# Dense 16-bit results from VectorE's last pass over its score blocks, with part of the work on GpSimd

## The chip, the cores and the metric

The kernel runs on one core of a Trainium2 chip. The time is device microseconds of one execution; a kernel's figure is the median of its runs. Five engines work side by side: TensorE (PE, with its weight loads as PEld), VectorE (DVE), ScalarE (ACT), GpSimd (POOL) and SyncE (SP), which here only issues DMA transfers.

## The reference

Two independent parts are computed and concatenated. Part A is multi-head attention with 32 heads of 16 channels over 2048 positions; part B is a long causal convolution with a gate.

```python
qkv = x @ wqkv                                   # A: x is 2048 x 512
scores = einsum("bhqd,bhkd->bhqk", q, k) * Dh**-0.5
p = softmax(scores)
a = einsum("bhqk,bhkd->bhqd", p, v) @ wo
k_shift = sum over 4 taps of shifted k * shift_k # B
kv = k_shift * v
y = causal convolution of kv with ssm_k (length 2048) + kv * ssm_D
b = q * y
return concatenate([a, b], axis=-1)              # bfloat16, 1 x 2048 x 1024
```

The exponentials of part A are 32 x 2048 x 2048 numbers. The kernel cuts them into 2048 **blocks** of 128 keys by 512 queries.

## The kernel before

**Chunks.** The program is written out by a planner that runs when the kernel is built. It walks over 695 chunks (index T). A chunk has two or three score blocks, each in a PSUM bank of its own: `emit_qk` issues one matmul for each block (L756) and then one ScalarE activation, exp from PSUM to the bf16 tile `PT` (L763). There are two groups of three banks, and odd and even chunks take turns. The matmuls of chunk T+1 may start when each of its banks is free, and a bank is free when its exp, or VectorE's first read of it, is done. Later `emit_pv` multiplies each block of exponentials with the values (L930).

**Who makes the exponentials.** ScalarE makes most of them. In some chunks `dve_choice` gives the last block to VectorE; ScalarE's activation then covers 1024 columns and not 1536 (in the first 56 chunks every second one has only two blocks to begin with). `dve_choice` says no where the planner's own clock has VectorE too far behind (`FIX_BEHIND`, `LATE`, `OPEN_LATE`), where a set was begun too recently (`OPEN_STEPS`, `APART`), or where the place for a result is still in use.

**How VectorE makes an exponential.** The scores come scaled so that a power of two has 2^16 steps. The block is first read out of PSUM as an int32 fixed-point number (`exp_on_dve`, L784, "fix" below; tiles `EI` and, later, a part of `xT`). After that it works on **sets** of two or four blocks (`Set`, `passes`), in SBUF:

- L815 `to_frac`: the low 16 bits, as f16: the fraction f. GpSimd makes it one block at a time where the planner finds a slot, otherwise VectorE does.
- L880, L882, L883, L885: four passes over the whole set, with f16 tiles (`EA`, or the lent tiles `WKV`, `STG`, `xT`, `YB`): a cubic correction with its two roots near 0 and 1.
- L886: the last pass, in pieces of half a set: the int32 number times 128, plus the correction, written back as int32. Its upper 16 bits are the bf16 exponential, and L930 reads every second 16-bit word.

**What sets the order.** Every engine takes its instructions in the order that the planner wrote. VectorE's fixes come when their chunk does. The passes wait in a list (`dve_fill`) from which the planner takes one whenever it thinks VectorE would be idle, and at the latest when the set's results are due. `free_slot` hands GpSimd one job for each VectorE instruction of about 0.69 us that reads PSUM (two for one of 1.24 us), with a wait for the VectorE instruction two places earlier; so a job stands ready when such an instruction begins. GpSimd's jobs are L815 and the softmax division L959. Other names in the profile: L484, L465, L510, L450, L1000, L1048, L1129 and L1147 are VectorE's reads of other matmul results, L536 and L542 prepare the convolution, L1116 is the convolution's matmul, L1293 and L1311 are matmuls with zeros that only fill TensorE's time.

Of the kernel before, what the change touches and what calls it, by code (L numbers as in the profile page):

```python
# [17 lines left out]
QB = 512  # L18
# [24 lines left out]
N_EARLY = 56  # L43
LAGS = 5
CONV_AT = 128
CONV_END = 650
TAIL = 18

OCT = 2.0 ** 16
ROOT0, ROOT1 = 0.0127173909, 0.9900476185
C0, C1 = 0.3043078141, 0.0780240431
FS = 128.0
BITS = 2.0 ** 23
QSCALE = SCALE * math.log2(math.e) * OCT
FIX_LO = -118.0 * OCT
FIX_ADD = 127.0 * OCT
# [28 lines left out]
HARD = 0.7  # L88
# [14 lines left out]
KZ_AT = 11  # L103
KZ0_AT = 14
DG_AT = (1, 1, 7, 8)
V_DUE = 1
PACE = 0.9
FULL_PARTS = 6
KZ_LANDS = 24.2
# [105 lines left out]
def bass_concat_heads__mha_block__ssm_conv_h3__prompt_kernel(  # L215
# [442 lines left out]
    def ei_of(off, n=1):  # L658
        return EI[:, off:off + n, :] if off < 8 else EIC[:, off - 8:off - 8 + n, :]
# [131 lines left out]
            full(s)  # L791
        return s.fix[-1]

    pool_jobs, waiting = [], []

    def full(s):
        if not s.pool:
# [15 lines left out]

    def to_frac(e, out, src):
        return e.tensor_scalar(out, src.bitcast(UINT16).rearrange("p i (f e) -> p i f e", e=2)[:, :, :, 0],  # L815
                               FS / OCT, -FS * ROOT0, ALU.mult, ALU.add)

    class Job:

# [3 lines left out]
    def frac_job(s, i):  # L823
        def run(eng, deps):
            _, eb, old = bufs(s)
            s.frac[i] = pool.op(lambda e: to_frac(e, eb[:, i:i + 1, :], ei_of(s.off + i)), deps + [s.fix[i], h_set[s.w]] + old, us=POOL_US)
            if s in waiting and len(s.frac) == s.k:
                passes(s)
        pool_jobs.append(Job(s, s.fix[i], lambda: not s.before or all(b in h_blk for b in s.before.blks), run))

    def free_slot(us=0.69):
        if us < 0.65:
            return
        n = dve.n - 2
        pool.t = max(pool.t, dve.t - us + DVE_OVER)
        for _ in range(int(us / 0.6)):
            j = next((j for j in pool_jobs if j.dep[1] <= n and j.ready()), None)
            if j:
                pool_jobs.remove(j)
                j.run(pool, [(dve.sem, n)])  # L840
                dve.t = max(dve.t, pool.t)

    def passes(s):
        ei = ei_of(s.off, s.k)
        ea, eb, old = bufs(s)
        eg = ea.bitcast(BF16)
# [9 lines left out]
        def piece(rate, make, deps, i0, i1, ends):  # L856
            us = 0.155 + 0.533 * (i1 - i0) / rate

            def run():
                h = dve.op(make(slice(i0, i1)), [st.get(i, h_set[s.w]) for i in range(i0, i1)] + (deps() if callable(deps) else deps), us=us, fill=True)  # L860
                for i in range(i0, i1):
                    st[i] = h
                if ends:
                    h_set[s.w] = h_ea[s.ea] = h
                    for x in s.blks[i0:i1]:
                        h_blk[x] = h
            return us, run, due, s

        def step(rate, make, deps=(), ends=False):
            width = s.k if s.pool and not ends else (s.k + 1) // 2  # L870
            for i0 in range(0, s.k, width):
                new.append(piece(rate, make, deps if callable(deps) else list(deps), i0, min(i0 + width, s.k), ends))

        make = lambda sl: lambda e: to_frac(e, eb[:, sl], ei[:, sl])
        if not s.frac:
            step(2, make, s.fix + old)
        for i in range(s.k):
            if s.frac and i not in s.frac:
                new.append(piece(2, make, s.fix + old, i, i + 1, False))
        step(4, lambda sl: lambda e: e.tensor_scalar(ea[:, sl], eb[:, sl], FS * (ROOT0 - ROOT1), None, ALU.add),  # L880
             lambda: [h_set[s.w], h_ea[s.ea]] + old)
        step(2, lambda sl: lambda e: e.tensor_tensor(ea[:, sl], ea[:, sl], eb[:, sl], ALU.mult))  # L882
        step(4, lambda sl: lambda e: e.tensor_scalar(eb[:, sl], eb[:, sl], C1 * BITS / FS ** 3,  # L883
                                                     (C0 + C1 * ROOT0) * BITS / FS ** 2, ALU.mult, ALU.add))
        step(2, lambda sl: lambda e: e.tensor_tensor(eg[:, sl], ea[:, sl], eb[:, sl], ALU.mult))  # L885
        step(1, lambda sl: lambda e: e.scalar_tensor_tensor(ei[:, sl], ei[:, sl], BITS / OCT, eg[:, sl], ALU.mult, ALU.add),  # L886
             ends=True)
# [26 lines left out]
    def emit_pv(bl, T):  # L914
# [676 lines left out]
```

## Time and profile before

| | |
|---|---|
| runs shown | 815.08, 816.94, 818.94 us; median 816.94 us |
| profiled execution | 814.36 us, of which the profile's span is 812.6 us |
| ACT busy | 796.1 us, 98% of the span, 702 instructions |
| DVE busy | 775.1 us, 95%, 1078 instructions |
| PE busy | 706.1 us, 87% |
| POOL busy | 354.9 us, 44%, 344 instructions |
| granted TensorE clock | full speed throughout |

A row of the groups reads: line, engine, operation, tiles written and read, shapes, count | total busy us, mean ns of one | idle time of the engine just before these instructions, and what ended it. Two instructions that follow each other on an engine overlap a little in these records, so durations add up to slightly more than time. A row of the timeline begins with start and duration in us.

### The profile page before, as it was taken

The page shows a single profiled execution, that of the slowest core. Times are in us where ns is not written, and L with a number is a line of the kernel's source. Part 1 is how long each engine was busy: PE and PEld are TensorE (multiplying, and loading weights), DVE is VectorE, ACT ScalarE, POOL GpSimd, SP SyncE. Part 2 cuts the span into 40 slices and gives each one's busy share as a digit, 9 for nine tenths or more (in the row PEclk, how much of TensorE's full clock was granted, in tenths as well). Part 3 has the DMA queues.
Part 4 walks back from the last instruction along what each step waited for, and adds up shares of the span by engine and source line. Part 5 has one row for each costly group of instructions (what it writes and reads, how often), then busy time and mean ns, then how long its engine had stood idle before and what let it go on. Part 6 is the DMA issues. An engine that isn't in the chain of part 4 may idle for free.

```text
span 812.6 us, 30077 instructions
## 1 busy us (share of the span) xinstructions
PE 706.1 (87%) x13348; PEld 316.5 (39%) x13383; DVE 775.1 (95%) x1078; ACT 796.1 (98%) x702; POOL 354.9 (44%) x344
## 2 busy tenths in 40 slices
PE   8998889888888889888888888888888888888897
PEld 3333334333334433343434343344444444344432
DVE  4999999999999999999999999999999999999996
ACT  7999999999999999999999999999999999999996
POOL 4202223244444464645534534345465556545450
PEclk9999999999999999999999999999999999999999
DMA  9986601115468775668767687787898999658810
GB/s 247 284 328 215 183 1 26 52 27 141 151 193 253 225 231 184 191 208 288 225 195 244 217 273 237 221 272 240 263 289 253 294 314 292 201 164 274 286 28 27
DMA packets 125010, 167.33 MB, mean 206 GB/s; under 512 B 50384, under 2 KB 57040, under 8 KB 124624
## 3 DMA queue, kind: packets, MB, share of 16 engines
q1 hardware_dynamic: 122480, 164.34, 65.8%
q8 instruction: 106, 1.74, 0.9%
q10 hardware_dynamic: 2400, 1.05, 0.5%
q14 instruction: 24, 0.20, 0.1%
HBM read 143.14 MB, written 16.52 MB: 196 GB/s over the span
## 4 chain that ended last, share of the span: by engine, by line
ACT 84%; DVE 8%; PE 6%; DMA 1%; issue 1%; POOL 0%; DVEq 0%
ACT PT L763 84%; PE PS L756 2%; DVE EI L886 1%; DVE EI L784 1%; PE PS L930 1%; DMA WR<-kz_scratch 1%; PE PS L474 1%; DVE EA L880 1%; DVE VAF L484 1%; DMA KV<-in_A_x_dram 1%; DVE WR L536 1%; DVE EA L882 0%; PE PS L498 0%; DVE EA L885 0%; DVE KV L510 0%
## 5 line engine op out<-in xcount | busy, mean ns | idle before, releaser
L763 ACT ACTIVATE PT<-PS 128x1024 bf16<-128x1024 f32 (+1 forms) x695 | 792.1, 1450 | 4.8 <-PE PS L756 4.0
L756 PE MATMUL PS<-QT,KTo 32*128 32x512 bf16 x2048 | 272.0, 384 | 89.8 <-ACT PT L763 63.1
L930 PE MATMUL PS<-PT,VAF 128*32 128x512 bf16 x1748 | 232.4, 389 | 2.0 <-DVE STG L1000 1.7
L1116 PE MATMUL PS<-WR,KV 128*18 128x64 bf16 (+15 forms) x8192 | 186.6, 213 | 1.3 <-DMA WR<-kz_scratch 0.8
L1116 PEld LDWEIGHTS PS<-WR,KV 128*18 128x18 bf16 (+15 forms) x8192 | 150.7, 119 | 40.4 <-issue 18.5
L756 PEld LDWEIGHTS PS<-QT,KTo 32*128 32x128 bf16 x2048 | 69.7, 91 | 241.0 <-ACT PT L763 215.7
L815 POOL TENSOR_SCALAR xT<-EI 128x512 f16<-128x512 uint16 x88 | 107.2, 1218 | 106.6 <-DVE EI L886 28.6
L784 DVE TENSOR_SCALAR EI<-PS 128x512 int32<-128x512 f32 x220 | 150.2, 684 | 3.7 <-PE PS L756 3.5
L815 POOL TENSOR_SCALAR STG<-EI 128x512 f16<-128x512 uint16 x76 | 84.1, 1106 | 86.6 <-DVE EI L886 23.3
L930 PEld LDWEIGHTS PS<-PT,VAF 128*32 128x32 bf16 x1748 | 55.2, 93 | 91.1 <-issue 84.0
L886 DVE SCALAR_TENSOR_TENSOR EI<-EI,EA 128x1024 int32<-128x1024 int32 (+1 forms) x92 | 90.2, 989 | 0.5
L815 POOL TENSOR_SCALAR xT<-xT 128x512 f16<-128x512 uint16 x40 | 43.7, 1092 | 47.0 <-DVE EI L886 25.7
L815 POOL TENSOR_SCALAR STG<-xT 128x512 f16<-128x512 uint16 x40 | 42.1, 1051 | 44.0 <-DVE EI L886 25.2
L1293 PE MATMUL PS<-ZR,IDN 128*128 128x512 bf16 (+3 forms) x217 | 59.3, 325 | 0.0
L930 PE MATMUL PS<-EI,VAF 128*32 128x512 bf16 x220 | 54.1, 406 | 2.0 <-DVE VAF L484 1.5
L784 DVE TENSOR_SCALAR xT<-PS 128x512 int32<-128x512 f32 x80 | 54.7, 684 | 0.2 <-PE PS L756 0.2
L886 DVE SCALAR_TENSOR_TENSOR EI<-EI,WKV 128x1024 int32<-128x1024 int32 x38 | 46.0, 1213 | 0.1
L882 DVE TENSOR_TENSOR EA<-EA,xT 128x2048 f16<-128x2048 f16 x32 | 39.7, 1240 | 0.3
L885 DVE TENSOR_TENSOR EA<-EA,xT 128x2048 bf16<-128x2048 f16 x32 | 39.0, 1220 | 0.4
L815 POOL TENSOR_SCALAR YB<-EI 128x512 f16<-128x512 uint16 x18 | 13.8, 767 | 54.2 <-DVE EI L784 30.9
L815 POOL TENSOR_SCALAR EA<-EI 128x512 f16<-128x512 uint16 x20 | 15.9, 794 | 48.8 <-DVE EI L784 10.4
L885 DVE TENSOR_TENSOR WKV<-WKV,STG 128x2048 bf16<-128x2048 f16 x29 | 35.3, 1219 | 0.5
(100 smaller groups left out, 644.1 us busy)
## 6 DMA issues: line engine op xcount, KB each, us to landing
WR<-kz_scratch SPq DMA_DIRECT2D x512, 256.0 KB, 3.8
kz_scratch<-WR SPq DMA_DIRECT2D x16, 752.0 KB, 4.3
QN<-in_B_q_dram SPq DMA_DIRECT2D x16, 128.0 KB, 3.3
out_dram<-KV SPq DMA_DIRECT2D x16, 128.0 KB, 4.0
out_dram<-OUTA SPq DMA_DIRECT2D x12, 128.0 KB, 1.9
QT<-in_B_ssm_k_dram SPq DMA_DIRECT2D x1, 1024.0 KB, 5.6
EI<-in_B_ssm_k_dram SPq DMA_DIRECT2D x1, 1024.0 KB, 8.8
STG<-in_B_v_dram SPq DMA_DIRECT2D x1, 1024.0 KB, 7.2
```

Source lines behind the costliest of these rows:

```text
L474: ins = e.matmul(PS[:, bank, 256 * i:256 * i + 256], lhsT=xT[:, dc, (kt + i) * 128:(kt + i + 1) * 128], rhs=WV[:, dc, 256 * z:256 * z + 25 ...
L484: bank_free[bank] = hh = dve.op(lambda e: e.tensor_copy(dst, src), [h, h_vaf1])
L756: ins = e.matmul(PS[:, bank, :], lhsT=KTo[32 * s:32 * s + 32, g // 2, kt * 128:(kt + 1) * 128], rhs=QT[32 * s:32 * s + 32, qb % 2, g, :], ...
L763: h_exp[T] = act.op(lambda e: e.activation(PT[:, T % R_PT, 0:n * QB], PS[:, banks[0]:banks[0] + n, :].rearrange("p b f -> p (b f)"), ACT.E ...
L784: s.fix.append(dve.op(lambda e: e.tensor_scalar(ei_of(i)[:, 0, :], PS[:, bank, :], FIX_LO, FIX_ADD, ALU.max, ALU.add), [h] + old + [o.pv[i ...
L815: return e.tensor_scalar(out, src.bitcast(UINT16).rearrange("p i (f e) -> p i f e", e=2)[:, :, :, 0], FS / OCT, -FS * ROOT0, ALU.mult, ALU ...
L882: step(2, lambda sl: lambda e: e.tensor_tensor(ea[:, sl], ea[:, sl], eb[:, sl], ALU.mult))
L885: step(2, lambda sl: lambda e: e.tensor_tensor(eg[:, sl], ea[:, sl], eb[:, sl], ALU.mult))
L886: step(1, lambda sl: lambda e: e.scalar_tensor_tensor(ei[:, sl], ei[:, sl], BITS / OCT, eg[:, sl], ALU.mult, ALU.add), ends=True)
L930: ins = e.matmul(PS[32 * s:32 * s + 32, pvb(qb * NG + g), :], lhsT=VAF[:, kt, h * VW:h * VW + 32], rhs=rhs, start=(order[b] == 0), stop=(o ...
L1116: ins = e.matmul(PS[32 * c:32 * c + NW - 2 * n, BGB, col:col + 64], lhsT=KV[:, 2 * n:NW, 4 * qd + c], rhs=w, start=(n == 0), stop=(n == NB ...
L1293: return e.matmul(PS[:, bank, col:col + 128 * k], lhsT=IDN[:, :], rhs=ZR[:, :].rearrange("p (m d) -> p m d", m=1).broadcast_to([128, 4 * k ...
```

## The change

The last pass no longer keeps the linear part of the number in int32. The four passes make the whole mantissa as a cubic in the fraction, f(C1 + f(C2 + f C3)), scaled to 128 steps, and the last pass adds the integer part times 128 and writes a dense int16 row, which is the bit pattern of the bf16 exponential (the first half of the block's int32 row). L966, the matmul with the values, reads that dense row.

The integer part is the upper 16 bits of the fixed-point number. It gets to the last pass in one of two ways. Where the planner finds a GpSimd slot before the last pass is issued, GpSimd makes the integer part times 128 as f16, one block at a time and in place (`to_whole`, L834; these `whole_jobs` come after `pool_jobs` in `free_slot`), and the last pass is a plain `tensor_tensor` add of two f16 rows (L884). Otherwise it is a `scalar_tensor_tensor` that reads the upper words itself (L889). If a piece has one block of each kind, it is cut into single blocks. Some of the planner's constants have new values.

```diff
-CONV_END = 650
+CONV_END = 640
-OPEN_STEPS = 4
+OPEN_STEPS = 5
-LATE = 8.0
+LATE = 9.0
-PAIRS_AT_END = 18
+PAIRS_AT_END = 20
-OPEN_LATE = 4.0
+OPEN_LATE = 5.0
-FIX_BEHIND = 1.6
+FIX_BEHIND = 1.7
-FIX_LATE = 0.4
+FIX_LATE = 0.45
-V_DUE = 1
+V_DUE = 0
-POOL_WAIT = 8
+POOL_WAIT = 7
+FINISH_RATE = 1.8
-X2_AT = 140
-X1_AT = 162
+X2_AT = 146
+X1_AT = 166
...
     def to_frac(e, out, src):
         return e.tensor_scalar(out, src.bitcast(UINT16).rearrange("p i (f e) -> p i f e", e=2)[:, :, :, 0],
-                               FS / OCT, -FS * ROOT0, ALU.mult, ALU.add)
+                               FS / OCT, None, ALU.mult)
...
+    def to_whole(e, out, src):
+        return e.tensor_scalar(out.bitcast(FP16)[:, :, 0:QB], src.bitcast(UINT16).rearrange("p i (f e) -> p i f e", e=2)[:, :, :, 1],
+                               FS, None, ALU.mult)
+
+    def whole_job(s, i, dep):
+        def run(eng, deps):
+            s.whole[i] = pool.op(lambda e: to_whole(e, ei_of(s.off + i), ei_of(s.off + i)),
+                                 deps + [dep, s.frac.get(i)], us=POOL_US)
+        whole_jobs.append(Job(s, dep, lambda: True, run))
...
-            j = next((j for j in pool_jobs if j.dep[1] <= n and j.ready()), None)
+            j = next((j for j in pool_jobs + whole_jobs if j.dep[1] <= n and j.ready()), None)
...
+                if k0 in s.whole:
+                    h = dve.op(lambda e: e.tensor_tensor(out, ei[:, sl].bitcast(FP16)[:, :, 0:QB], m, ALU.add),
+                               [st[i] for i in range(k0, k1)] + [s.whole[i] for i in range(k0, k1)],
+                               us=0.155 + 0.533 * (k1 - k0) / 2, fill=True)
+                else:
+                    whole = ei[:, sl].bitcast(UINT16).rearrange("p i (f e) -> p i f e", e=2)[:, :, :, 1]
+                    h = dve.op(lambda e: e.scalar_tensor_tensor(out, whole, FS, m, ALU.mult, ALU.add),
+                               [st[i] for i in range(k0, k1)], us=0.155 + 0.533 * (k1 - k0), fill=True)
...
-        step(4, lambda sl: lambda e: e.tensor_scalar(ea[:, sl], eb[:, sl], FS * (ROOT0 - ROOT1), None, ALU.add),
+        step(4, lambda sl: lambda e: e.tensor_scalar(ea[:, sl], eb[:, sl], C3 / FS ** 2, C2 / FS, ALU.mult, ALU.add),
              lambda: [h_set[s.w], h_ea[s.ea]] + old)
         step(2, lambda sl: lambda e: e.tensor_tensor(ea[:, sl], ea[:, sl], eb[:, sl], ALU.mult))
-        step(4, lambda sl: lambda e: e.tensor_scalar(eb[:, sl], eb[:, sl], C1 * BITS / FS ** 3,
-                                                     (C0 + C1 * ROOT0) * BITS / FS ** 2, ALU.mult, ALU.add))
-        step(2, lambda sl: lambda e: e.tensor_tensor(eg[:, sl], ea[:, sl], eb[:, sl], ALU.mult))
-        step(1, lambda sl: lambda e: e.scalar_tensor_tensor(ei[:, sl], ei[:, sl], BITS / OCT, eg[:, sl], ALU.mult, ALU.add),
-             ends=True)
+        step(4, lambda sl: lambda e: e.tensor_scalar(ea[:, sl], ea[:, sl], C1, None, ALU.add))
+        step(2, lambda sl: lambda e: e.tensor_tensor(ea[:, sl], ea[:, sl], eb[:, sl], ALU.mult))
+        for i0 in range(0, s.k, (s.k + 1) // 2):
+            new.append(finish(i0, min(i0 + (s.k + 1) // 2, s.k)))
...
-                rhs = ei_of(on_dve[b][1])[:, 0, :].bitcast(BF16).rearrange("p (f e) -> p f e", e=2)[:, :, 1] if b in on_dve else PT[:, Tc % R_PT, j * QB:(j + 1) * QB]
+                rhs = ei_of(on_dve[b][1]).bitcast(BF16)[:, 0, 0:QB] if b in on_dve else PT[:, Tc % R_PT, j * QB:(j + 1) * QB]
```

What the planner makes of it, counted over the whole program (lines of the new kernel in brackets):

| instructions | before | after |
|---|---|---|
| ACT, exp over 1536 columns | 358 | 352 |
| ACT, exp over 1024 columns | 337 | 343 |
| DVE, fix L784 (L785) | 300 | 306 |
| DVE, passes over a set of four, 2048 columns | 65 sets | 66 sets |
| DVE, passes over a set of two, 1024 columns (or 2 x 512) | 20 sets | 21 sets |
| DVE, last pass L886 (L889), scalar_tensor_tensor: pairs / single blocks | 130 / 40 | 71 / 44 |
| DVE, last pass (L884), tensor_tensor: pairs / single blocks | none | 26 / 68 |
| DVE, fraction L815 (L816) of one block | 2 | 24 |
| POOL, fraction L815 (L816) of one block | 298 | 282 |
| POOL, integer part (L834) of one block | none | 120 |
| POOL, division L959 (L995) | 23 | 23 |
| DVE, all instructions | 1078 | 1152 |

By chunk, blocks on VectorE go from 39 to 40 in the first 128 chunks and from 261 to 266 after them. Up to the 40th fix the last passes were 35 single scalar_tensor_tensor; now they are 29 single tensor_tensor and 5 single scalar_tensor_tensor.

The order on VectorE in the opening (sets of two blocks), where a set ends and the next begins, at about the 26th fix. Before:

```order
L885 TENSOR_TENSOR EA<-EA 128x1024 [waits s_dve]
L484 CAST VAF<-PS 128x2x16x16 [waits s_pe]
L886 SCALAR_TENSOR_TENSOR EI<-EI,EA 128x512 [waits s_dve]
L886 SCALAR_TENSOR_TENSOR EI<-EI,EA 128x512
L880 TENSOR_SCALAR EA<-YB 128x1024 [waits s_dve,s_pool]
L484 CAST VAF<-PS 128x2x16x16 [waits s_pe]
L784 TENSOR_SCALAR EI<-PS 128x512 [waits s_pe]
L882 TENSOR_TENSOR EA<-EA,YB 128x1024 [waits s_dve]
```

The same engine and place in the changed kernel:

```order
L785 TENSOR_SCALAR EI<-PS 128x512 [waits s_pe]
L884 TENSOR_TENSOR EI<-EI,EA 128x512 [waits s_pool,s_dve]
L785 TENSOR_SCALAR EI<-PS 128x512 [waits s_pe] x2
L884 TENSOR_TENSOR EI<-EI,EA 128x512 [waits s_pool]
L917 TENSOR_SCALAR EA<-YB 128x1024 [waits s_dve,s_pool]
L785 TENSOR_SCALAR EI<-PS 128x512 [waits s_pe]
L919 TENSOR_TENSOR EA<-EA,YB 128x1024 [waits s_dve]
```

Both last passes of the set now wait for GpSimd (`s_pool`), and two fixes stand between them. Waits for GpSimd on VectorE, over the program, go from 98 to 171; 84 of them are on L884.

The order on GpSimd at about the same place, before:

```order
L815 TENSOR_SCALAR EA<-EI 128x512 [waits s_dve] x2
L959 TENSOR_TENSOR OB<-STG,DR 128x2x8x16 [waits s_dve] x2
L815 TENSOR_SCALAR YB<-EI 128x512 [waits s_dve] x2
L815 TENSOR_SCALAR EA<-EI 128x512 [waits s_dve] x2
L815 TENSOR_SCALAR YB<-EI 128x512 [waits s_dve] x2
L815 TENSOR_SCALAR EA<-EI 128x512 [waits s_dve] x2
```

And in the changed kernel:

```order
L995 TENSOR_TENSOR OB<-STG,DR 128x2x8x16 [waits s_dve] x2
L816 TENSOR_SCALAR EA<-EI 128x512 [waits s_dve]
L834 TENSOR_SCALAR EI<-EI 128x512 [waits s_pool]
L816 TENSOR_SCALAR EA<-EI 128x512 [waits s_dve]
L834 TENSOR_SCALAR EI<-EI 128x512 [waits s_pool,s_dve]
L816 TENSOR_SCALAR YB<-EI 128x512 [waits s_dve] x2
L834 TENSOR_SCALAR EI<-EI 128x512 [waits s_pool,s_dve]
L816 TENSOR_SCALAR EA<-EI 128x512 [waits s_dve] x2
```

Nearly every block of the opening brings GpSimd a second job, which stands in its queue between the fractions.

More of the change, by code (lines that the diff above doesn't have):

```diff
@@ L11 @@
 UINT16 = mybir.dt.uint16
+INT16 = mybir.dt.int16
 FP16 = mybir.dt.float16
@@ L635, in __init__ @@
             self.frac, self.passed = {}, False
+            self.whole, self.split = {}, {}
             self.over = [s for s in sets if s.off < off + k and off < s.off + s.cap]
@@ L792, in exp_on_dve @@
         return s.fix[-1]
[L794 removed]
+    pool_jobs, whole_jobs, waiting = [], [], []
     def full(s):
@@ L862, in run, with finish, one @@
                     st[i] = h
[L863 to L866, printed above, removed]
+                    if split and s.pool:
+                        whole_job(s, i, h)
             return us, run, due, s
-        def step(rate, make, deps=(), ends=False):
-            width = s.k if s.pool and not ends else (s.k + 1) // 2
+        def finish(i0, i1):
+            def one(k0, k1):
+                sl = slice(k0, k1)
+                out, m = ei[:, sl].bitcast(INT16)[:, :, 0:QB], ea[:, sl]
+                if k0 in s.whole:
[6 more added lines that the diff above has]
+                               [st[i] for i in range(k0, k1)], us=0.155 + 0.533 * (k1 - k0), fill=True)
+                for i in range(k0, k1):
+                    st[i] = h
+                h_set[s.w] = h_ea[s.ea] = h
+                for x in s.blks[k0:k1]:
+                    h_blk[x] = h
+            def run():
+                whole_jobs[:] = [j for j in whole_jobs if j.of is not s or not i0 <= j.i < i1]
+                if len({i in s.whole for i in range(i0, i1)}) == 1:
+                    one(i0, i1)
+                else:
+                    for i in range(i0, i1):
+                        one(i, i + 1)
+            return 0.155 + 0.533 * (i1 - i0) / FINISH_RATE, run, due, s
@@ L871, in step @@
+        def step(rate, make, deps=(), split=False):
+            width = s.k if s.pool else (s.k + 1) // 2
             for i0 in range(0, s.k, width):
-                new.append(piece(rate, make, deps if callable(deps) else list(deps), i0, min(i0 + width, s.k), ends))
+                new.append(piece(rate, make, deps if callable(deps) else list(deps), i0, min(i0 + width, s.k), split))
         make = lambda sl: lambda e: to_frac(e, eb[:, sl], ei[:, sl])
         if not s.frac:
-            step(2, make, s.fix + old)
+            step(2, make, s.fix + old, split=True)
```

13 lines of the change are left out of this document (6 added, 7 removed).

## The prediction

> **What bounds the kernel now.** I read the page first: the busy shares, then the chain of waits followed back from the end.
>
> ```profile
> PE 706.1 (87%) x13348; PEld 316.5 (39%) x13383; DVE 775.1 (95%) x1078; ACT 796.1 (98%) x702; POOL 354.9 (44%) x344
> ACT 84%; DVE 8%; PE 6%; DMA 1%; issue 1%; POOL 0%; DVEq 0%
> L763 ACT ACTIVATE PT<-PS 128x1024 bf16<-128x1024 f32 (+1 forms) x695 | 792.1, 1450 | 4.8 <-PE PS L756 4.0
> ```
>
> ScalarE is busy 796.1 of 812.6 us, and 84% of the chain is its exponentials. In front of all 695 of them it was idle for only 4.8 us. So the time is the number of blocks on ScalarE, plus those 4.8 us, plus a head and a tail. VectorE, at 95%, is close behind. Next I asked where the idle time lies: busy time before and after 160 us (PE, PEld, DVE, ACT, POOL), then the exponentials of the first 160 us alone.
>
> ```profile
> 0.00:160.00 160.00, 140.43 (x1175) 54.74 (x1187) 145.64 (x260) 150.41 (x136) 41.52 (x65) 1.00 0.58 170
> 160.00:800.00 640.00, 556.85 (x12135) 259.34 (x12154) 623.53 (x805) 639.64 (x561) 313.39 (x279) 1.00 0.71 218
> ...
> L763 ACT ACTIVATE PT<-PS 128x1536 bf16<-128x1536 f32 x63 | 89.7, 1499 | 2.6 <-PE PS L756 2.4
> L763 ACT ACTIVATE PT<-PS 128x1024 bf16<-128x1024 f32 x68 | 68.4, 1070 | 1.8 <-PE PS L756 1.6
> ```
>
> From 160 us on ScalarE is idle 0.36 us of 640: there only fewer blocks can help. VectorE has 640 - 623.5 = 16.5 us free there. Before 160 us ScalarE waits 2.6 + 1.8 = 4.4 us for scores. One such wait, in the timeline:
>
> ```profile
> 78.91 0.62 POOL L959 TENSOR_TENSOR OB<-STG,DR 128x256 bf16<-128x256 f32 x1 [2.12 <-DVE EI L886]
> 78.96 0.85 DVE L880 TENSOR_SCALAR EA<-YB 128x1024 f16<-128x1024 f16 x1
> 79.73 1.28 DVE L784 TENSOR_SCALAR EI<-PS 128x512 int32<-128x512 f32 x2
> 80.56 0.39 PE L756 MATMUL PS<-QT,KTo 32*128 32x512 bf16 x3 [0.68 <-DVE EI L784]
> 80.99 1.45 ACT L763 ACTIVATE PT<-PS 128x1536 bf16<-128x1536 f32 x1 [0.60 <-PE PS L756]
> ```
>
> A GpSimd job begins 0.05 us ahead of a VectorE pass; the pass takes 0.85 us instead of 0.42; the fix behind it frees its bank late; the scores come late; ScalarE stands for 0.60 us. This chain is what the change can shorten (less work in front of the fix) or lengthen (more GpSimd jobs).
>
> **The change part by part.** *ScalarE.* Six activations of 1536 columns become 1024.
>
> ```profile
> L763 ACT ACTIVATE PT<-PS 128x1536 bf16<-128x1536 f32 x358 | 571.2, 1660 | 2.8 <-PE PS L756 2.4
> L763 ACT ACTIVATE PT<-PS 128x1024 bf16<-128x1024 f32 x337 | 400.1, 1228 | 1.9 <-PE PS L756 1.6
> ```
>
> 6 x (1.660 - 1.228) = **2.6 us** off the engine that sets the end. VectorE pays for the six blocks, so its balance decides whether they come free.
>
> *VectorE.* The rows with its prices:
>
> ```profile
> L784 DVE TENSOR_SCALAR EI<-PS 128x512 int32<-128x512 f32 x220 | 150.2, 684 | 3.7 <-PE PS L756 3.5
> L886 DVE SCALAR_TENSOR_TENSOR EI<-EI,EA 128x1024 int32<-128x1024 int32 x52 | 63.1, 1216 | 0.2
> L886 DVE SCALAR_TENSOR_TENSOR EI<-EI,WKV 128x1024 int32<-128x1024 int32 x38 | 46.0, 1213 | 0.1
> L886 DVE SCALAR_TENSOR_TENSOR EI<-EI,EA 128x512 int32<-128x512 int32 x40 | 27.1, 694 | 0.3
> L886 DVE SCALAR_TENSOR_TENSOR xT<-xT,EA 128x1024 int32<-128x1024 int32 x20 | 24.2, 1212 | 0.1
> L886 DVE SCALAR_TENSOR_TENSOR xT<-xT,WKV 128x1024 int32<-128x1024 int32 x20 | 24.2, 1217 | 0.1
> ...
> L880 DVE TENSOR_SCALAR EA<-EA 128x1024 f16<-128x1024 f16 x10 | 5.2, 517 | 0.5
> L882 DVE TENSOR_TENSOR EA<-EA,YB 128x1024 f16<-128x1024 f16 x9 | 6.2, 685 | 0.1
> L885 DVE TENSOR_TENSOR EA<-EA,YB 128x1024 bf16<-128x1024 f16 x9 | 6.2, 684 | 0.1
> L880 DVE TENSOR_SCALAR EA<-YB 128x1024 f16<-128x1024 f16 x9 | 4.7, 521 | 0.4
> L883 DVE TENSOR_SCALAR YB<-YB 128x1024 f16<-128x1024 f16 x9 | 3.8, 425 | 0.2
> ...
> L885 DVE TENSOR_TENSOR EA<-EA 128x512 bf16<-128x512 f16 x2 | 0.8, 422 | 0.0
> L815 DVE TENSOR_SCALAR EA<-EI 128x512 f16<-128x512 uint16 x2 | 0.8, 420 | 0.0
> ...
> L880 DVE TENSOR_SCALAR EA<-xT 128x2048 f16<-128x2048 f16 x32 | 22.4, 701 | 0.2
> L882 DVE TENSOR_TENSOR EA<-EA,xT 128x2048 f16<-128x2048 f16 x32 | 39.7, 1240 | 0.3
> ```
>
> Last pass before: 63.1 + 46.0 + 27.1 + 24.2 + 24.2 = 184.6 us. After: 71 pairs and 44 singles of scalar_tensor_tensor at the old prices, 71 x 1.215 + 44 x 0.694 = 116.8. The trace has no f16 add into int16; the nearest rows are the f16 products L885, 0.684 for a pair and 0.422 for a single block: 26 x 0.684 + 68 x 0.422 = 46.5. Together 163.3, **21.3 us less**. Bounds for the add: that price, or the 1.215 and 0.694 of L886 (14 + 18 = 32 us more, a rival below); L882 and L885 write different 16-bit types at one price, so I take the first.
>
> Against it: 22 more fractions on VectorE, 22 x 0.420 = 9.2; six more fixes, 6 x 0.684 = 4.1; a set of two more, 0.52 + 0.69 + 0.43 + 0.68 = 2.3; a set of four more, with L885 priced as L882 and L883 no dearer than L880, 0.70 + 1.24 + 0.70 + 1.24 = 3.9. That is +19.5: 1.8 us less in all. There are 74 more instructions, and neighbours overlap in the records:
>
> ```profile
> 403.28 0.68 DVE L784 TENSOR_SCALAR xT<-PS 128x512 int32<-128x512 f32 x1
> 403.88 1.22 DVE L885 TENSOR_TENSOR EA<-EA,xT 128x2048 bf16<-128x2048 f16 x1
> 405.01 0.69 DVE L880 TENSOR_SCALAR WKV<-STG 128x2048 f16<-128x2048 f16 x1
> 405.62 0.69 DVE L784 TENSOR_SCALAR xT<-PS 128x512 int32<-128x512 f32 x1
> ```
>
> 403.28 + 0.68 is 0.08 past the next start, so 74 x 0.08 = 5.9 us of the durations are no time. VectorE's own work falls by **7.7 us**, nearly all of it in the opening, where 29 single blocks change from 0.694 to 0.422 (7.9 us). The passes in between keep their number, widths and order, so the cubic itself costs nothing more.
>
> *GpSimd.* 120 integer parts are added and 16 fractions leave: 104 jobs more.
>
> ```profile
> L815 POOL TENSOR_SCALAR EA<-EI x20: 617/714/1121, 13.8 to 156.7; 128x512 f16<-128x512 uint16 x20
> DVE MSK L387 <- POOL IDN L367: 0.4, 1, 0.4
> ```
>
> Alone a job takes 0.617 us (min, median, max in ns), about one fix; the longer ones stood blocked behind a pass. The second row is the only wait of VectorE for GpSimd in the list of waits. So today's 98 waits cost nothing as idle time, and the price hides in longer passes: L880, the pass behind the fraction, takes 0.517 and 0.521 where L883 takes 0.425, so (10 x 0.092 + 9 x 0.096) = 1.8 us over the 38 fraction jobs of those sets, 0.047 each. I take this: 104 x 0.047 = **+4.9 us** on VectorE. Bounds: nothing (the job falls wholly under a fix), or 0.43 each (0.85 against 0.42 above) = 45 us. VectorE's net is then -2.8 us: the six blocks come free, with no more to spare than now from 160 us on.
>
> The Trainium skill (SBUF — State Buffer, § Who interferes with whom and § SBUF: two separate sides) has GpSimd and VectorE share one pair of SBUF ports as an exclusive lock held for a whole instruction, against VectorE passes in a two-port mode or with two SBUF inputs. The stretched L880 agrees. By it both kinds of last pass shut GpSimd out, and 425 jobs of 0.617 us (262 us) must fit beside VectorE's reads of PSUM. It speaks against this change, and is the mechanism of the first rival.
>
> *Early waits.* Of the 4.4 us I take **1.2 us** back: the opening has 6 us less work on VectorE (7.9, less 29 x 0.047 and one more fraction), but the first 56 chunks give it 12 blocks and not 10, and some waits are for TensorE. Bounds: 0 and 4.4. *TensorE* reads 306 rows densely; it is 87% busy and bounds nothing, so I count nothing.
>
> **Sum.** 814.36 (the profiled execution: 812.6 span and 1.8 around it) - 2.6 - 1.2 = 810.6. The median of the runs lies 2.6 above that execution, so **813.1 us** as a median, 0.5% down.
>
> **Rivals.**
> - *GpSimd's jobs collide (slower).* Place: after 160 us, 75 of the 104 jobs. Price: each delays a pass, and the fix behind it. It decides from 16.5 / 75 = 0.22 us a job, when VectorE's free time there is used up. At 0.34, halfway to the 0.43 seen, 25.5 - 16.5 = 9.0, less 2.6: 823 us. For it: ACT's idle 0.60 above, and 84 passes that newly wait for GpSimd. Against: 0.047 a job so far. 10%.
> - *The add into int16 runs at the old rate (slower).* After the opening 26 pairs and 39 singles cost 26 x 0.531 + 39 x 0.272 = 24.4 more, 7.9 over the free time, and the opening loses its 7.9, of which half may reach ScalarE: 816.9 - 2.6 + 7.9 + 4 = 826 us. Against: one price for two output types. 4%. (The Trainium skill, VectorE: DVE Perf Modes, § What auto-detection actually checks, lets the two-a-cycle mode go with 16-bit types and step 1, which this add has; no row shows it for int16.)
> - *All early waits go.* -2.6 - 4.4 = -7.0: 809.9 us. For it: the chain above starts from VectorE. Against: part of those waits is for other engines. 15%.
> - *The saving is lost again to new early waits* of 2 to 4 us, since the opening is dealt out anew: 817 us, no change. 18%.
>
> **Numbers.** My forecast has 53%, with its own range 810.5 to 815.5. A run of this kernel can tell 0.5%, 4.1 us: faster means under 812.9. The forecast lies on that edge; with a bit under half of it and the third rival, faster 0.39; its rest and the fourth, same 0.47; the first two, slower 0.14. Eight in ten: 808.5 to 819.5 us.
>
> **What would show it.** Right: ACT 352 and 343 exps with idle in front of them under 4.8 us; L884 near 0.68 and 0.42; L917 on 1024 columns not much over 0.52; DVE busy within 10 us of 775. Wrong: L884 near 1.2; passes stretched by 0.2 us or more on average behind L834; VectorE idle on GpSimd for several us; ScalarE idle after 160 us.

## The result: 935 us instead of 817

| | before | after |
|---|---|---|
| median (lowest to highest, 6 runs each) | 817.0 us (815.08 to 818.94) | 935.21 us (929.36 to 939.75) |
| ratio, 95% interval | | 1.144 [1.139, 1.150] |
| profiled execution, span | 814.36, 812.6 us | 939.75, 937.8 us |

The change costs 118 us. The forecast was 813.1 us with a range to 819.5; it was wrong, and not by a little. The page of the changed kernel: busy time of the engines, granted TensorE clock in 40 slices, the chain of waits by engine, and the groups that matter.

```profile
PE 758.5 (81%) x13316; PEld 326.1 (35%) x13351; DVE 803.7 (86%) x1152; ACT 814.6 (87%) x702; POOL 748.2 (80%) x448
...
PEclk9899979979788898789999999899997978899799
...
POOL 37%; DVE 35%; PE 14%; issue 9%; ACT 5%; POOLq 0%; DVEq 0%
...
L764 ACT ACTIVATE PT<-PS 128x1024 bf16<-128x1024 f32 (+1 forms) x695 | 810.4, 1260 | 111.3 <-PE PS L757 105.2
...
L757 PE MATMUL PS<-QT,KTo 32*128 32x512 bf16 x2048 | 296.4, 419 | 114.3 <-DVE EI L785 56.1
...
L834 POOL TENSOR_SCALAR EI<-EI 128x512 f16<-128x512 uint16 x99 | 174.1, 1768 | 35.1 <-DVE EI L884 9.1
...
L816 POOL TENSOR_SCALAR xT<-EI 128x512 f16<-128x512 uint16 x86 | 153.2, 1797 | 26.3 <-DVE EI L889 9.7
```

ScalarE's exponentials were 84% of the chain; now ScalarE is 5% of it and GpSimd, which had 0%, is 37%. GpSimd is busy 748.2 us and was busy 354.9. ScalarE stands 111.3 us ahead of its exponentials (4.8 before). VectorE's work did not grow enough to explain that: 803.7 against 775.1. The list of waits says how the time travels:

```profile
ACT PT L764 <- PE PS L757: 105.2, 142, 4.7
...
PE PS L757 <- DVE EI L785: 56.1, 90, 3.7
...
DVE EI L884 <- POOL EI L834: 23.0, 22, 3.4
...
PE PS L757 <- DVE xT L785: 19.3, 29, 2.0
...
DVE WKV L917 <- POOL STG L816: 15.2, 10, 3.8
DVE EA L917 <- POOL xT L816: 14.7, 12, 2.1
```

(Engine and line that waited, engine and line waited for, us in total, times, longest.) Read from GpSimd up: VectorE waits for the integer parts (L834) and for the fractions (L816); the fixes (L785) queued behind those waits come late; the scores (L757) have no free bank; ScalarE waits for scores. All of VectorE's waits for GpSimd add up to 76 us, where there was 0.4. One such chain in the timeline:

```profile
302.77 1.49 POOL L834 TENSOR_SCALAR EI<-EI 128x512 f16<-128x512 uint16 x1
302.86 1.59 DVE L921 TENSOR_TENSOR EA<-EA,xT 128x2048 f16<-128x2048 f16 x1
304.23 1.57 POOL L816 TENSOR_SCALAR STG<-EI 128x512 f16<-128x512 uint16 x1
305.93 0.69 DVE L917 TENSOR_SCALAR WKV<-STG 128x2048 f16<-128x2048 f16 x1 [1.48 <-POOL STG L816]
306.54 0.42 DVE L884 TENSOR_TENSOR EI<-EI,EA 128x512 int16<-128x512 f16 x1
...
307.48 0.69 DVE L785 TENSOR_SCALAR xT<-PS 128x512 int32<-128x512 f32 x1
...
308.32 0.61 PE L757 MATMUL PS<-QT,KTo 32*128 32x512 bf16 x3
...
308.98 1.02 ACT L764 ACTIVATE PT<-PS 128x1024 bf16<-128x1024 f32 x1 [2.51 <-PE PS L757]
```

Two GpSimd jobs of about 1.5 us stand one behind the other, VectorE stops for 1.48 us ahead of L917, the fix (L785) and the scores (L757) follow late, and ScalarE, which stood for 2.51 us, goes on 3 us after VectorE did. What is odd here is the 1.49 and the 1.57. Of the kernel before I had read that a job alone takes 0.617 us. The shortest of each kind in the changed kernel (min, median and max in ns):

```profile
L834 POOL TENSOR_SCALAR EI<-EI x99: 1482/1647/2490, 17.2 to 861.8; 128x512 f16<-128x512 uint16 x99
...
L816 POOL TENSOR_SCALAR EA<-EI x20: 1482/1488/1976, 14.7 to 171.2; 128x512 f16<-128x512 uint16 x20
```

Not one job is under 1.478 us. L816 is the job that was L815: same tile, same types, same size, and its *minimum* went from 617 to 1482 ns. Waiting for another engine would rather spread the durations and leave the minimum where it was: in the kernel before, the same jobs ran from 617 to 1677 ns. So the instruction itself looks like a dearer one, and the diff has one thing about it that changed: `to_frac` had a multiplication and an addition, and now has a multiplication alone. `to_whole` has a multiplication alone too.

### The profile page after: what moved, and what is told of

Its sections match the earlier page's. It is cut to its first block, busy times and chain, and to the rows that moved or that the text cites. A ratio compares the mean times of both kernels' runs of the same rounds, so it can differ in the third digit from the quotient of the medians.

```text
span 937.8 us, 30352 instructions
## 1 busy us (share of the span) xinstructions
PE 758.5 (81%) x13316; PEld 326.1 (35%) x13351; DVE 803.7 (86%) x1152; ACT 814.6 (87%) x702; POOL 748.2 (80%) x448
## 4 chain that ended last, share of the span: by engine, by line
POOL 37%; DVE 35%; PE 14%; issue 9%; ACT 5%; POOLq 0%; DVEq 0%
POOL EI L834 10%; POOL xT L816 10%; POOL STG L816 8%; DVE EI L785 5%; PE PS L757 5%; ACT PT L764 5%; DVE EI L889 4%; PE PS L966 4%; POOL xT L834 3%; DVE EA L919 3%; DVE xT L889 2%; DVE EA L921 2%; DVE EA L917 2%; DVE EI L884 2%; POOL YB L816 2%
## 5 line engine op out<-in xcount | busy, mean ns | idle before, releaser
L764 ACT ACTIVATE PT<-PS 128x1024 bf16<-128x1024 f32 (+1 forms) x695 | 810.4, 1260 | 111.3 <-PE PS L757 105.2
L757 PE MATMUL PS<-QT,KTo 32*128 32x512 bf16 x2048 | 296.4, 419 | 114.3 <-DVE EI L785 56.1
L966 PE MATMUL PS<-PT,VAF 128*32 128x512 bf16 x1742 | 254.5, 425 | 1.0 <-DVE STG L1036 0.6
L834 POOL TENSOR_SCALAR EI<-EI 128x512 f16<-128x512 uint16 x99 | 174.1, 1768 | 35.1 <-DVE EI L884 9.1
L1152 PE MATMUL PS<-WR,KV 128*8 128x64 bf16 (+15 forms) x8192 | 193.4, 218 | 2.1 <-DMA WR<-kz_scratch 0.6
L816 POOL TENSOR_SCALAR xT<-EI 128x512 f16<-128x512 uint16 x86 | 153.2, 1797 | 26.3 <-DVE EI L889 9.7
L1152 PEld LDWEIGHTS PS<-WR,KV 128*12 128x12 bf16 (+15 forms) x8192 | 152.3, 120 | 55.8 <-issue 37.6
L757 PEld LDWEIGHTS PS<-QT,KTo 32*128 32x128 bf16 x2048 | 73.0, 92 | 264.3 <-ACT PT L764 148.6
L785 DVE TENSOR_SCALAR EI<-PS 128x512 int32<-128x512 f32 x226 | 153.2, 682 | 5.0 <-PE PS L757 4.6
L816 POOL TENSOR_SCALAR STG<-EI 128x512 f16<-128x512 uint16 x72 | 136.1, 1904 | 25.9 <-DVE xT L889 10.5
L966 PEld LDWEIGHTS PS<-PT,VAF 128*32 128x32 bf16 x1742 | 56.0, 95 | 97.0 <-issue 90.7
L966 PE MATMUL PS<-EI,VAF 128*32 128x512 bf16 x226 | 63.3, 424 | 26.8 <-DVE EI L884 16.0
L816 POOL TENSOR_SCALAR xT<-xT 128x512 f16<-128x512 uint16 x37 | 70.7, 1926 | 15.4 <-DVE EI L889 8.4
L816 POOL TENSOR_SCALAR STG<-xT 128x512 f16<-128x512 uint16 x36 | 66.5, 1861 | 14.9 <-DVE EA L921 4.1
L785 DVE TENSOR_SCALAR xT<-PS 128x512 int32<-128x512 f32 x80 | 54.6, 682 | 4.6 <-PE PS L757 4.6
L884 DVE TENSOR_TENSOR EI<-EI,EA 128x512 int16<-128x512 f16 (+1 forms) x61 | 32.9, 549 | 16.2 <-POOL EI L834 16.0
L889 DVE SCALAR_TENSOR_TENSOR EI<-EI,EA 128x1024 int16<-128x1024 uint16 (+1 forms) x47 | 44.9, 959 | 0.3
L834 POOL TENSOR_SCALAR xT<-xT 128x512 f16<-128x512 uint16 x21 | 38.8, 1853 | 6.8 <-DVE xT L884 2.4
L921 DVE TENSOR_TENSOR EA<-EA,xT 128x2048 f16<-128x2048 f16 x33 | 42.6, 1291 | 0.2
L919 DVE TENSOR_TENSOR EA<-EA,xT 128x2048 f16<-128x2048 f16 x33 | 41.8, 1267 | 0.2
L816 POOL TENSOR_SCALAR YB<-EI 128x512 f16<-128x512 uint16 x19 | 29.5, 1561 | 14.9 <-DVE EI L785 7.0
```

The source lines that it names most:

```text
L757: ins = e.matmul(PS[:, bank, :], lhsT=KTo[32 * s:32 * s + 32, g // 2, kt * 128:(kt + 1) * 128], rhs=QT[32 * s:32 * s + 32, qb % 2, g, :], ...
L764: h_exp[T] = act.op(lambda e: e.activation(PT[:, T % R_PT, 0:n * QB], PS[:, banks[0]:banks[0] + n, :].rearrange("p b f -> p (b f)"), ACT.E ...
L785: s.fix.append(dve.op(lambda e: e.tensor_scalar(ei_of(i)[:, 0, :], PS[:, bank, :], FIX_LO, FIX_ADD, ALU.max, ALU.add), [h] + old + [o.pv[i ...
L834: return e.tensor_scalar(out.bitcast(FP16)[:, :, 0:QB], src.bitcast(UINT16).rearrange("p i (f e) -> p i f e", e=2)[:, :, :, 1], FS, None, ...
L884: h = dve.op(lambda e: e.tensor_tensor(out, ei[:, sl].bitcast(FP16)[:, :, 0:QB], m, ALU.add), [st[i] for i in range(k0, k1)] + [s.whole[i] ...
L889: h = dve.op(lambda e: e.scalar_tensor_tensor(out, whole, FS, m, ALU.mult, ALU.add), [st[i] for i in range(k0, k1)], us=0.155 + 0.533 * (k ...
```

## The experiments

Two theories. *Form*: on GpSimd a `tensor_scalar` with one operation is slower than one with two, and all else follows from 402 dear jobs. *Number*: the first rival of the prediction; 104 jobs more collide with VectorE's passes and make each other late, and the long records are jobs that were shut out.

**The mended kernel, e1_two_op.** The changed kernel, with an addition of zero in both jobs, so that the order on every engine is the same.

```diff
 def to_frac ...
-                               FS / OCT, None, ALU.mult)
+                               FS / OCT, 0.0, ALU.mult, ALU.add)
 def to_whole ...
-                               FS, None, ALU.mult)
+                               FS, 0.0, ALU.mult, ALU.add)
```

> The changed kernel with a second operation in both of GpSimd's passes (times a constant, plus 0.0, in place of the multiplication alone); every engine's order and every wait stay word for word. Theory A (GpSimd's pass with one operation takes 1.48 us where the pass with two took 0.617, and everything else follows from that): L816 and L834 fall to a minimum of 0.62 us, VectorE's waits for GpSimd (some 80 us in the changed kernel) go to under 5 us, ScalarE's idle time in front of its exponentials from 111 us to 3 to 6 us, and the time to that of the prediction, 809 to 817 us. Theory B (104 more jobs collide with VectorE's passes over the memory ports, and the long durations are time spent blocked): nothing changes but rounding, 925 to 940 us.

Measured: 816.05 us (812.84 to 823.14, 12 runs) beside 816.12 for the kernel before; ratio 1.0009 [0.9981, 1.0037]. The 118 us are gone. Its page:

```profile
span 813.8 us, 30352 instructions
...
PE 702.1 (86%) x13316; PEld 316.0 (39%) x13351; DVE 767.5 (94%) x1152; ACT 795.4 (98%) x702; POOL 410.5 (50%) x448
...
ACT 58%; DVE 23%; PE 5%; issue 4%; POOL 3%; DVEq 0%; POOLq 0%
```

And the row of its integer parts, to set against the one above:

```profile
L834 POOL TENSOR_SCALAR EI<-EI x99: 614/727/1657, 15.8 to 742.8; 128x512 f16<-128x512 uint16 x99
```

An operation more took the shortest L834 from 1.482 to 0.614 us. GpSimd's busy time falls by 337.7 us from 748.2, which is 0.84 us for each of 402 jobs. VectorE waits 0.4 us for GpSimd, as before the change, with the same 448 instructions on GpSimd. *Number* is out: the same jobs in the same order at the old price bring no wait for GpSimd, and the time is that of the kernel before.

**The kernel before, with one operation, e2_before_one_op.** The same edit the other way: nothing of the change but the dropped addition.

```diff
-                               FS / OCT, -FS * ROOT0, ALU.mult, ALU.add)
+                               FS / OCT, None, ALU.mult)
```

> The kernel before, with only the addition taken out of the fraction pass (the root's shift is left out, so the exponentials are off by about a hundredth of an octave's position; same order, same waits, same count of jobs, none added). Theory A: the 298 fraction jobs go from 0.617 to 1.48 us at the least, 257 us more on GpSimd, 355 to some 610 us busy; VectorE begins to wait for them; 840 to 900 us. Theory B: the count of jobs is as before, so 815 to 819 us.

Measured: 863.91 us (two runs), ratio 1.058 [1.054, 1.062]. The busy shares on its page:

```profile
PE 724.0 (84%) x13348; PEld 322.2 (37%) x13383; DVE 789.8 (92%) x1078; ACT 807.8 (94%) x702; POOL 587.8 (68%) x344
```

And two rows of its list of waits:

```profile
DVE EA L880 <- POOL xT L815: 14.9, 11, 2.3
DVE WKV L880 <- POOL STG L815: 13.3, 12, 2.0
```

298 dear jobs put 233 us on GpSimd, and VectorE's first pass, which never waited for a fraction, now does. So a loss of this kind, 48 us here, needs neither the new passes nor the new order.

**One kind of job at a time, e3_fraction_two_op and e4_integer_two_op.** The first of the two edits of e1 alone, then the second alone.

> The changed kernel with the second operation (plus 0.0) in the fraction pass alone; the integer part stays with one operation. Theory A: L816 at 0.62 us, L834 still at 1.48; 120 x 0.86 = 103 us of the excess of 345 us on GpSimd remain, and the waits that remain are those of L884 for L834; 835 to 865 us. Theory B: 925 to 940 us.

> The changed kernel with the second operation (plus 0.0) in the integer pass alone; the fraction stays with one operation. Theory A: L834 at 0.62 us, L816 at 1.48; 282 x 0.86 = 243 us of the excess remain; 870 to 915 us, more than the run with the fraction mended. Theory B: 925 to 940 us.

| kernel (one profile each) | dear jobs | time | GpSimd busy | VectorE's waits for GpSimd | TensorE's for fixes (L757) | ScalarE's ahead of exps |
|---|---|---|---|---|---|---|
| before | 0 | 814.4 | 354.9 | 0.4 | 9.8 | 4.0 |
| e1, both cheap | 0 | 815.6 | 410.5 | 0.4 | 21.8 | 6.0 |
| e3, integer parts dear | 120 | 853.2 | 517.1 | 27.8 | 45.6 | 30.8 |
| e2, before with dear fractions | 298 | 861.9 | 587.8 | 30.5 | 59.7 | 38.7 |
| e4, fractions dear | 282 | 877.4 | 642.3 | 40.1 | 65.2 | 54.1 |
| after, both dear | 402 | 939.8 | 748.2 | 76.2 | 75.4 | 108.0 |

(Time is that of the profiled execution; e3 and e4 have no other. The three wait columns are sums over the list of waits, in us.) In the order of the changed kernel (e1, e3, e4, after) every step of the chain grows with the dear jobs. VectorE's own work on the same 1152 instructions grows with them too: 767.5 us busy in e1, 781.3 in e3, 794.4 in e4 and 803.7 after. The dear GpSimd jobs thus reach ScalarE in two ways, as waits (76 us after) and as longer passes (36 us more than in e1). The 120 integer parts cost 38 us and the 282 fractions 62 us; together they cost 124, more than the sum. By the job the integer parts are the dearer (0.31 us against 0.22); why, was not tried.

**The price by itself, e7_gpsimd_alone.** GpSimd alone runs `tensor_scalar` on 128x512, each form several times. L43 has one operation, L44 two.

```python
        if op1 is None:
            return lambda e: e.tensor_scalar(dst, src, a, None, op0)    # L43
        return lambda e: e.tensor_scalar(dst, src, a, b, op0, op1)      # L44
```

> GpSimd alone, all else left out (the output is zeros): tensor_scalar over 128x512, four times each: low 16-bit words to f16 with one multiplication, then with a multiplication and an addition; the same two for f32 to f32 and for f16 to f16; then words to f16 with one addition, and with an addition and a multiplication. Theory A: 1.48 against 0.62 us for the words with nothing else running. Whether the type matters is open: if one operation takes a slower routine for every type, all pairs show a factor over two; if it is the conversion from 16-bit integers, only the words do. Theory B: 0.62 us for all.

Its groups by form:

```profile
L43 POOL TENSOR_SCALAR DSTH<-WORD 128x512 f16<-128x512 uint16 x8 | 11.9, 1491 | 0.7
L43 POOL TENSOR_SCALAR DSTF<-FULL 128x512 f32<-128x512 f32 x4 | 5.9, 1487 | 0.3
L43 POOL TENSOR_SCALAR DSTH<-HALF 128x512 f16<-128x512 f16 x4 | 5.9, 1487 | 0.3
L44 POOL TENSOR_SCALAR DSTH<-WORD 128x512 f16<-128x512 uint16 x8 | 4.9, 617 | 0.7
L44 POOL TENSOR_SCALAR DSTH<-HALF 128x512 f16<-128x512 f16 x4 | 2.5, 617 | 0.3
L44 POOL TENSOR_SCALAR DSTF<-FULL 128x512 f32<-128x512 f32 x4 | 2.5, 617 | 0.3
```

With no other engine at work, and for three pairs of types, one operation takes 1.49 us and two take 0.617. In the rows of `WORD` half the instructions multiply (first) and half add (first); it makes no difference. *Form* is shown, and contention is no part of this price. In the changed kernel it comes on top: the groups of its page have means of 1.56 to 1.93 us where the shortest job takes 1.48. Why GpSimd is built so, no run here tells.

What is left to explain is e1: mended, the change still gains nothing, where the sum had 3.8 us off. Four more kernels ask where those went.

**Without the integer jobs, e6_no_integer_jobs.** e1, and `whole_job` returns at once, so that every last pass is a `scalar_tensor_tensor`.

```diff
     def whole_job(s, i, dep):
+        return
```

> The changed kernel with two operations in the fraction pass, its own constants, and no integer part on GpSimd: every last pass is scalar_tensor_tensor. The planner gives VectorE 300 blocks, as before. If the integer part on GpSimd is what buys the blocks: ScalarE's work is that of the kernel before, 816 to 821 us, with GpSimd's count of jobs back near 300 and VectorE's passes less stretched. If the jobs cost more in collisions than they save: under 815 us.

Measured: 822.59 us, ratio 1.0068 [1.0041, 1.0095]. The planner gives VectorE 300 blocks again, as before, and the last passes sum to 184.0 us (184.6 before; in e1, with 306 blocks, L884 and L889 have 161.3). So the dense result by itself saves VectorE nothing, and the plain adds behind GpSimd's integer parts save it 22.7 us. With them the time is 6.5 us shorter (e1 against e6; 0.6% by the two ratios). This part of the change does what it says once its job is cheap. That e6 is slower than the kernel before, and than the 816 to 821 us expected, is another matter. The planner leaves 31 fractions to VectorE, where it made 2, which is 29 x 0.42 = 12 us (e5 below, with the old constants, leaves 5), and 10.0 us lie behind ScalarE's last exponential, against 7.7 before; what share each has was not tried.

**The old constants, e5_old_constants, and with a longer end, e8_old_pairs24.** e1 with the eleven changed constants of the planner as they were, then the same with sets of two instead of four over a longer stretch at the end. (The constants are gathered into two lines here.)

```diff
-CONV_END, OPEN_STEPS, LATE, PAIRS_AT_END, OPEN_LATE = 640, 5, 9.0, 20, 5.0
-FIX_BEHIND, FIX_LATE, V_DUE, POOL_WAIT, X2_AT, X1_AT = 1.7, 0.45, 0, 7, 146, 166
+CONV_END, OPEN_STEPS, LATE, PAIRS_AT_END, OPEN_LATE = 650, 4, 8.0, 18, 4.0    # e8: PAIRS_AT_END = 24
+FIX_BEHIND, FIX_LATE, V_DUE, POOL_WAIT, X2_AT, X1_AT = 1.6, 0.4, 1, 8, 140, 162
```

> The changed kernel with two operations in both of GpSimd's passes, and the planner's eleven changed constants back at their old values. The planner then gives VectorE 312 blocks (300 before, 306 in the changed kernel), so ScalarE has 346 and 349 exponentials: 12 x 0.427 = 5.1 us less than the kernel before. Theory C (the changed kernel, mended, only equals the kernel before because its constants let VectorE run later, and that gave back in waits what six blocks saved): idle time in front of the exponentials stays near 5 us and the time is 810 to 814 us. Theory D (VectorE is full, so any block more comes back as waits): idle 8 to 12 us, 815 to 820 us.

> Two operations in both GpSimd passes and the planner's old constants, but sets of two already from the 24th chunk before the end (18 before), so that the last set on VectorE is one of two blocks and not one of four. VectorE gets 310 blocks: 10 x 0.427 = 4.3 us less on ScalarE than in the kernel before. In the run with all old constants ScalarE's last exponential ended 0.7 us earlier than in the kernel before, but 11.2 us of span came behind it and not 7.7, because the last set's passes ended 3 us after it. Theory C (the tail took the gain): the stretch behind the last exponential is 7 to 8 us again, and the time 811 to 815 us. Theory D (every block more comes back as waits): 816 to 820 us.

Measured: e5 818.39 us, ratio 1.0023 [1.0007, 1.0039]; e8 816.35 us, 0.9996 [0.9978, 1.0015]. The planner gave VectorE 312 blocks in e5 and 310 in e8 (300 before, 306 in e1), and ScalarE's busy time fell to 792.1 and 793.4 from 796.1. The time did not follow: e5 is even 0.2% longer, and both fell where the second theory had them. In e5 part of the reason stands at the end of the timeline:

```profile
804.88 2.36 DVE L889 SCALAR_TENSOR_TENSOR EI<-EI,WKV 128x1024 int16<-128x1024 uint16 x2
...
807.38 0.61 PE L966 MATMUL PS<-EI,VAF 128*32 128x512 bf16 x4 [2.25 <-DVE EI L889]
...
810.32 0.60 ACT L1097 ACTIVATE QT<-PS 128x512 bf16<-128x512 f32 x1 [6.17 <-PE PS L1077]
```

ScalarE's last exponential is done at 804.1 us, but VectorE's last set only at 807.2, and everything behind it is late: 11.2 us from the last exponential to the end, against 7.7 before. e8 shortens that to 8.7. Both have the rest of their loss ahead of the exponentials: ScalarE waits 7.1 us for scores in e5 and 7.3 in e8, against 4.0 before.

**Only the constants on lateness, e9_old_lateness.** e1 with five constants as before (308 blocks; gathered into one line here).

```diff
-OPEN_STEPS, LATE, OPEN_LATE, FIX_BEHIND, FIX_LATE = 5, 9.0, 5.0, 1.7, 0.45
+OPEN_STEPS, LATE, OPEN_LATE, FIX_BEHIND, FIX_LATE = 4, 8.0, 4.0, 1.6, 0.4
```

> Two operations in both GpSimd passes; of the changed constants the five that say how late VectorE may run (LATE, OPEN_LATE, OPEN_STEPS, FIX_BEHIND, FIX_LATE) are back at the old values, the other six stay changed. VectorE gets 308 blocks: 8 x 0.427 = 3.4 us less on ScalarE. If the looser constants made the fixes late (TensorE waited 19 us for fixes after 160 us in the mended kernel, 8 us before), those waits fall to about 8 to 10 us, ScalarE's idle time in front of its exponentials to 4 to 5 us, and the time is 811 to 815 us. If not, waits and time stay near those of the mended kernel: 815 to 818 us.

Measured: 815.22 us, ratio 0.9985 [0.9968, 1.0002], with 7.6 us at the end and 5.2 us of waits ahead of the exponentials (its profile is of its shortest run, 813.07 us). TensorE's waits for fixes after 160 us fall to 14.6 us from 19.4, not to the 8 to 10 expected, so the looser constants explain a part at most. It is the best of the set, and its interval still reaches no change. No version here is shown to beat the kernel before.

## Why the prediction was wrong, step by step

**The step that failed** is the part on *GpSimd*: "Alone a job takes 0.617 us", taken from the row of L815 and carried to all of the jobs of the changed kernel. The row was right for what it showed, an instruction with two operations. The changed job has one, and takes 1.48. The diff shows the dropped addition, and the part on *VectorE* passed by it with "the cubic itself costs nothing more": true of the four passes, but the cubic also took the root's shift out of the fraction, which is GpSimd's job. The term was +4.9 us with bounds of 0 and 45, and e1 against the changed kernel puts it at 119. Both bounds priced how jobs of the old length collide; neither asked whether the job itself had the old length.

The cost is not 402 x 0.87 us, since GpSimd had half of its time free. It came through the chain in the waits above and through VectorE's longer passes, and once GpSimd is late for one pass, the fixes behind that pass are late as well.

**The first rival** gave the right sign (823 us, 10%) for another mechanism. (The halfway price it meant, between 0.22 and 0.43, is 0.325 and not 0.34; that gives 822.) e1 has its 104 jobs, and VectorE waits 0.4 us. What collisions cost VectorE shows in the groups of e1, the pass behind a fraction (L917) beside the like pass that is not (L920):

```profile
L889 DVE SCALAR_TENSOR_TENSOR EI<-EI,EA 128x1024 int16<-128x1024 uint16 x24 | 29.2, 1217 | 0.3
...
L920 DVE TENSOR_SCALAR EA<-EA 128x2048 f16<-128x2048 f16 x36 | 25.1, 697 | 0.4
L917 DVE TENSOR_SCALAR EA<-xT 128x2048 f16<-128x2048 f16 x33 | 23.9, 725 | 0.4
L917 DVE TENSOR_SCALAR WKV<-STG 128x2048 f16<-128x2048 f16 x30 | 23.7, 789 | 1.2 <-issue 0.3
L920 DVE TENSOR_SCALAR WKV<-WKV 128x2048 f16<-128x2048 f16 x30 | 20.7, 689 | 0.4
L884 DVE TENSOR_TENSOR EI<-EI,EA 128x512 int16<-128x512 f16 x47 | 18.9, 417 | 0.3
...
L884 DVE TENSOR_TENSOR EI<-EI,EA 128x1024 int16<-128x1024 f16 x14 | 9.5, 684 | 0.1
```

33 x 0.028 + 30 x 0.100 = 3.9 us, and 1.3 on the sets of two: 5.2 us of stretch. The same sum over the groups of the kernel before is 2.5. But e6, which has no integer jobs at all, has 4.3 (its L919 is e1's L917, its L922 e1's L920):

```profile
L919 DVE TENSOR_SCALAR EA<-xT 128x2048 f16<-128x2048 f16 x32 | 24.9, 779 | 0.9
L922 DVE TENSOR_SCALAR EA<-EA 128x2048 f16<-128x2048 f16 x35 | 24.2, 692 | 0.4
L919 DVE TENSOR_SCALAR WKV<-STG 128x2048 f16<-128x2048 f16 x30 | 22.2, 740 | 0.5
L922 DVE TENSOR_SCALAR WKV<-WKV 128x2048 f16<-128x2048 f16 x30 | 20.9, 697 | 0.3
```

So the jobs added 2.7 us at most, and perhaps only 0.9: no more than the 4.9 taken, and far from 45. The Trainium skill (SBUF — State Buffer, § SBUF: two separate sides) describes the lock by which one of the two engines wholly blocks the other. The stretched passes agree with it, and at the old length of the jobs its price here is this small.

**The add into int16**: the rows above have 0.684 and 0.417 where 0.684 and 0.422 were taken. All of L884 in e1 sums to 45.4 us (46.5 in the forecast), and L889 to 115.9 (116.8). That rival is out, and "L884 near 0.68 and 0.42" was right where GpSimd is in time. In the changed kernel as it was timed the pairs take 0.80 to 0.83, which I read as being caught behind long jobs.

**VectorE's balance**: -2.8 us in the forecast; e1 has 767.5 against 775.1, -7.6. The sign held and there was more to spare than I thought.

**ScalarE's six blocks**: the counts are as planned, 352 and 343. But -2.6 us did not arrive. In e1, the exponentials, then busy time by stage (before and after 160 us; PE, PEld, DVE, ACT, POOL):

```profile
L764 ACT ACTIVATE PT<-PS 128x1024 bf16<-128x1024 f32 (+1 forms) x695 | 791.4, 1366 | 7.0 <-PE PS L757 6.0
...
0.00:160.00 160.00, 140.69 (x1165) 54.55 (x1175) 138.86 (x264) 150.07 (x136) 63.45 (x98) 1.00 0.59 170
160.00:800.00 640.00, 551.72 (x12101) 258.70 (x12125) 624.40 (x879) 637.43 (x559) 347.09 (x351) 1.00 0.71 218
```

From 160 us on ScalarE is idle 2.57 us, where it was 0.36: this is what "ScalarE idle after 160 us" was to warn of. VectorE has 15.6 us free in that stretch, but not at the right moments. The list of waits has TensorE's score matmuls wait 21.8 us for fixes, against 9.8, and in the chain of waits VectorE has 23% where it had 8%.

**Early waits**: -1.2 us in the forecast; they did not shrink. Before 160 us ScalarE stands 4.4 us ahead of its exponentials in e1, and stood 4.4 before. The opening of e1 has a large one that was not there before; in its timeline:

```profile
38.53 0.54 DVE L536 COPY WR<-QT 128x1440 bf16<-128x1440 bf16 x1 [2.40 <-DMA kz_scratch<-WR]
...
40.05 0.68 DVE L484 CAST VAF<-PS 128x512 bf16<-128x512 f32 x1
...
41.76 1.02 ACT L764 ACTIVATE PT<-PS 128x1024 bf16<-128x1024 f32 x1 [1.93 <-PE PS L757]
```

VectorE reaches a copy of the convolution before the DMA that must free its tile, stands 2.40 us, and ScalarE stands 1.93 us a little later. In time order that is VectorE first; that the one caused the other is read from the timeline, not tried. In e5 and e9, which share the old constants on lateness, the early waits are 3.2 us, so the 1.2 us of the forecast arrive there; but ScalarE then stands 4.3 us (e5) and 2.6 us (e9) ahead of its exponentials after 160 us, against 0.4 before.

With its price mended, then, the change ends at the time that the fourth rival gave (817 us, no change; measured 816.05, ratio 1.0009), but not by its mechanism. That rival had the saving lost to new early waits; the early ones stayed at 4.4 us, and the new ones came after 160 us. Idle time ahead of the exponentials is 7.0 us over the whole program and not under 4.8, and ScalarE's busy time fell by 0.7 us and not by 2.6. The second part I read as the same waits in another place, since records of exponentials that follow each other overlap and those behind a wait do not; that is argued, not shown. e5, e8 and e9 say the same from another side: 8 to 12 blocks less on ScalarE come back as waits or as a longer end.

One thing stays open here. The 12 runs of e1 fall into two groups by the granted TensorE clock: six at 0.998 or more take 812.8 to 815.6 us (median 813.9), six at 0.987 to 0.994 take 816.5 to 823.1. Of the 17 runs of the kernel before, 13 are at 0.998 or more, with a median of 816.0. So at the full clock e1 is some 2 us shorter, and it loses that clock in 6 of 12 runs against 4 of 17. Whether the lower clock lengthens those runs or only goes along with more waits, no run here tells; nor whether a better order could keep the saving.

## What to carry to other kernels

Price an instruction by its whole form, the number of its operations included, and look for each row of the old trace that a step reuses whether the diff touches that very instruction. When an engine's records get longer, look at the minimum first: a raised minimum points to a dearer instruction, a raised median with the old minimum to contention. Work taken off the engine that sets the end is worth its price only if the engine that takes it over can also be on time; here two engines at 94% and 98% gave none of it back.

## What the runs showed of the hardware that was not expected

- On GpSimd a `tensor_scalar` of 128x512 with one operation takes 1.49 us and with two 0.617, for uint16 to f16, f16 and f32, whether it multiplies or adds. The Trainium skill (GPSIMD Engine Reference, § 3.1 Elementwise — side-by-side cycle accounting) gives 769 ns as a best case for 512 elements; the measured forms lie on both sides of it. VectorE shows no such thing in its f16 passes: at 2048 columns its one-operation pass (L920) takes 0.697 and 0.689 us, and the two-operation pass of the kernel before (L883) 0.688 and 0.694.
- The granted TensorE clock fell with the waits: 0.904 over the changed kernel, 0.96 to 0.97 in e2, e3 and e4, 0.998 in e1 (profiled runs). The mean score matmul took 419 ns in the changed kernel and 384 in e1. It comes along with an idler TensorE (busy 81% of the span, 86% in e1) and goes when GpSimd's jobs are cheap again; how much of the 118 us is due to it was not separated.
